# Squared-ReLU attention and a PReLU feed-forward layer on one core: the order of the work written anew, stage by stage

## The chip, the core and the metric

The kernel runs on one core of one Trainium2 chip. A core has five engines that run side by side and wait for each other through semaphores: TensorE (PE in the profile; its weight loads are listed apart as PEld), VectorE (DVE), ScalarE (ACT), GpSimd (POOL) and SyncE (SP). Each engine takes its own instructions strictly in the order in which the program issues them. The metric is device time in microseconds, the median of several executions; less is better.

## The reference

Eight batches, twelve heads, 448 positions, head width 64. Then a feed-forward layer over all 8 x 448 = 3584 rows of width 768, inner width 2048:

```python
scores = scale * np.matmul(q, k.transpose(0, 1, 3, 2))
attn = np.maximum(scores, 0.0) ** 2 / S
x = np.matmul(attn, v)          # heads side by side: 3584 x 768
h = x @ w_in
g = np.maximum(h, 0.0) + alpha * np.minimum(h, 0.0)
return g @ w_out
```

There is no softmax: a score is rectified, squared and used.

## The kernel before

Twelve heads make three *quads* of four heads per batch, 24 quads in all (numbers 0 to 23). Rows of a head are split as 64 x 7, so that a quad's scores come in seven *chunks*.

One chunk is made in three steps. `score_mm` (L199) issues four 64x448 products on 64x64 tiles of TensorE (L204) into a pair of PSUM banks. `relu` (L210) rectifies them into an `rl` buffer, on ScalarE (L213, letter A) or VectorE (L215, letter D). `square` (L218) squares that into an `at` buffer, on VectorE (L226) or ScalarE (L224). A chunk that is rectified but not squared stands in the list `late`; `sq(k, eng)` squares the first k of it. There are six `rl` and ten `at` buffers.

When a quad's seven chunks are squared, `attnv` (L229) multiplies them with v: 28 products on 64x64 tiles (L236) into a pair of banks, which ScalarE (L246) and VectorE (L247) scale into `xT`. Three quads fill `xT` of one batch.

Layer one of the feed-forward part runs in 16 *units* per batch (`f1`, L281): six full-array products (L270) into one bank, then on ScalarE the negative part (L276) and on VectorE the sum (L277) into `gT`, and one square (`sq(1)`).

Layer two works on rows of 128 over two batches. For the first rows it is done plainly (`f2`, L294, products at L301). For the others, `Pair` (L316) computes two row blocks of 128 with seven products of half size instead of eight, from sums and differences of operands (`mix`, L332 on VectorE; `weight_mix`, L314, once for the weights). `p1` to `p7` are the seven products (L336); `p1` and `p2` share a bank that is held in between, as do `p5` and `p3`. Results are added on VectorE (`plus`, L341) or copied on ScalarE (L352, L357), and `store` (L286) writes each piece with two transfers of 64 rows.

q and k of a quad must be transposed. The first five quads are turned on TensorE (`turn_pe`, L171, products at L178, copies at L181). The others are copied into one buffer, `perm`, or a spare part of `w_mix`, on ScalarE or VectorE (L190), and turned by a transfer on SyncE's queue (`turn_dma`, L192). A one-element copy on GpSimd (L508 and others, `landed`) waits for that transfer; the loads that GpSimd issues stand behind it. `prepare` does both and issues the loads of later quads.

PSUM has eight banks. `take_bank` and `take_pair` give out the one or the pair that was taken longest ago; after L652 `one` prefers the neighbour of the bank that was given out last. A bank is free again when the engine that reads it is done.

The order in which all this is issued is written out by hand. Quads 0 to 5 and the first two batches have a list of calls of their own (L413 to L649). From L656 a loop runs over batches 2 to 7. In each batch layer one's 16 units come first, with three chunks before unit 9 (`FB`, L553) and with two quads prepared on ScalarE at units 4 and 12. Then the pairs' products follow, broken by three `burst`s (L565): three chunks, `attnv`, two or three chunks. Squares are issued on VectorE, in groups. At the very start 28 products of the identity with itself (L162) keep TensorE busy until data arrive.

I call a *visit* a run of products on 64x64 tiles (chunks or `attnv`) between full-array products.

Of the kernel before, what the change touches and what calls it, by code (L numbers as in the profile page):

```python
# [10 lines left out]
F32 = mybir.dt.float32  # L11
# [5 lines left out]
NJ = 7  # L17
# [3 lines left out]
def kernel(  # L21
# [43 lines left out]
    beta_sb = singles.tile([128, KF], F32)  # L65
    landed = singles.tile([1, 1], BF16)
# [4 lines left out]
    paired = []  # L71
# [77 lines left out]

    load_k0(0, FIRST)  # L150
# [9 lines left out]
    warm = psum[:, 7, :128]  # L160
    for _ in range(28):
        nc.tensor.matmul(warm, ident, ident, start=True, stop=True)  # L162
# [66 lines left out]
    def attnv(n, eng="AD"):  # L229
# [16 lines left out]
        nc.scalar.activation(xT[b][:, g, 0], ps[:, 0, :S], ACTF.Copy, scale=out_scale)  # L246
        nc.vector.tensor_scalar(xT[b][:, g, 1], ps[:, 1, :S], out_scale, None, ALU.mult)  # L247

    late = []

    def sc(chunks):

        for n, j, eng in chunks:
            late.append((n, j, relu(score_mm(n, j), eng)))

    def sq(k=99, eng="D"):
        for g in late[:k]:
            square(*g, eng)
        del late[:k]

    def run(chunks):
        sc(chunks)
        sq()
# [10 lines left out]
    def f1_out(ps, b, ff):  # L274
        neg = neg_pool.tile([128, S], F32, tag="neg", name="neg")
        nc.scalar.activation(neg, ps, ACTF.Relu, scale=-1.0)  # L276
        nc.vector.scalar_tensor_tensor(gT[:, ff, (b % 2) * S:(b % 2) * S + S],  # L277
                                       neg, beta_sb[:, ff:ff + 1], ps, ALU.mult, ALU.add)
        sq(1)

    def f1(b, ff):  # L281
        ps = take_bank()[:, :S]
        f1_mm(ps, b, ff, range(KM))
        f1_out(ps, b, ff)

    def store(sb, c, lo, hi, t, other=None):  # L286
        for u in range(2):
            blk = 2 * c + u
            b, j = 2 * sb + blk // NJ, blk % NJ
            rows = out[b * S:(b + 1) * S].rearrange("(pp j) d -> j pp d", j=NJ)  # L290
            eng = other if u and other else nc.sync
            eng.dma_start(out=rows[j][:, lo:hi], in_=t[64 * u:64 * u + 64])
# [23 lines left out]
    class Pair:  # L316
# [22 lines left out]
        def plus(self, ps, u, keep=None):  # L339
            t = keep or o_pool.tile([128, d_model - CUT], F32, tag="o", name="osb")[:, :u.shape[-1]]  # L340
# [42 lines left out]

        def p3(self):
# [5 lines left out]
    pat = "ADAAAAA"  # L390

    def ch(n, lo, hi, p=pat):
        return [(n, j, p[j]) for j in range(lo, hi)]

    early = {}
    todo = [(ff, km) for ff in range(4) for km in range(4)]

    def some_early(count):
        for ff, km in todo[:count]:
            if ff not in early:  # L400
                early[ff] = hold()
            f1_mm(psum[:, early[ff], :S], 0, ff, (km,))
        del todo[:count]

    def sq_of(n, j, eng):
        for g in [g for g in late if g[:2] == (n, j)]:
            square(*g, eng)
            late.remove(g)

# [4 lines left out]
    load_w_in(0)  # L414
    load_v(2)
    cast0(0, 2, "D")
    cast0(4, 6, "A")
    cast0(2, 4, "D")
    cast0(6, 7, "A")
    turn_pe(0, (("q", 0, 2, "D"),))  # L420
    turn_pe(0, (("q", 4, 6, "A"),))
    turn_pe(0, (("q", 2, 4, "D"),))
    turn_pe(0, (("q", 6, 7, "A"),))
    turn_pe(0, (("k", 0, 1, "D"),))
    turn_pe(0, (("k", 1, 2, "A"),))
    turn_pe(0, (("k", 2, 4, "D"),))
    sc([(0, 0, "A")])
    sc([(0, 1, "D")])
    turn_pe(0, (("k", 4, 7, "D"),))
    load_qk(3)  # L430
    load_w_in(1)
    load_w_in(2)
    sq_of(0, 0, "D")
    sc([(0, 2, "A")])
    sc([(0, 3, "A")])
    sq_of(0, 1, "D")
    turn_pe(1, (("q", 0, 7, "D"),))
    sc([(0, 4, "A")])
    sc([(0, 5, "A")])
    turn_pe(1, (("k", 0, 7, "D"),))  # L440
    load_qk(4)
    load_w_in(3)
    sq_of(0, 2, "D")
    sq_of(0, 5, "D")
    sc([(0, 6, "A")])
    sq_of(0, 4, "D")
    sq_of(0, 6, "D")
    sc([(1, 0, "A")])
    sq_of(0, 3, "D")
    sc([(1, 1, "A")])  # L450
    sc([(1, 2, "D")])
    sc([(1, 3, "A")])
    sc([(1, 4, "A")])
    sq_of(1, 0, "D")
    turn_pe(2, (("k", 0, 5, "D"),))
    turn_pe(2, (("q", 0, 7, "D"),))
    sq_of(1, 2, "D")
    sq_of(1, 4, "D")
    turn_pe(2, (("k", 5, 7, "A"),))
    load_w_out(0, 0, 8)  # L460
    load_qk(5)
    load_v(3)
    load_w_out(0, 8)
    load_v(4)
    load_v(5)
    sc([(1, 5, "A")])
    sc([(1, 6, "A")])
    sc([(2, 0, "A")])
    sc([(2, 1, "A")])
    sq_of(1, 1, "D")  # L470
    sq_of(1, 5, "D")
    sq_of(1, 3, "D")
    sq_of(1, 6, "D")
    attnv(0, "AD")
    sc([(2, 2, "A")])
    attnv(1, "AD")
    sc([(2, 3, "A")])
    sc([(2, 4, "D")])
    sq_of(2, 0, "A")
    some_early(11)  # L480
    sq_of(2, 4, "A")
    sc([(2, 5, "A")])
    sq_of(2, 1, "D")
    sq_of(2, 3, "D")
    sq_of(2, 2, "D")
    sc([(2, 6, "D")])
    sq_of(2, 5, "A")
    some_early(5)
    sq_of(2, 6, "D")
    nc.vector.tensor_scalar(beta_sb, alpha_sb, -1.0, 1.0, ALU.mult, ALU.add)  # L490
    attnv(2, "AD")
    some_early(0)
    turn_pe(3, (("q", 0, 7, "D"),))
    turn_pe(3, (("k", 0, 7, "D"),))
    for ff in range(4):
        f1_mm(psum[:, early[ff], :S], 0, ff, range(4, KM))
        f1_out(psum[:, early[ff], :S], 0, ff)
        take(early[ff], 1)


    def f1s(b, lo, hi):
        for ff in range(lo, hi):
            f1(b, ff)

    def prepare(n):
        if n < NQ:
            turn_dma(n)
            nc.gpsimd.tensor_copy(landed, T[n][:1, 0, 0, :1])  # L508
# [4 lines left out]

    f1s(0, 4, 6)
    sc(ch(3, 0, 3))
    f1s(0, 6, 8)
    sc(ch(3, 3, 6))
    f1s(0, 8, 9)
    ps = take_bank()[:, :S]
    f1_mm(ps, 0, 9, range(KM))  # L520
    turn_pe(4, (("q", 0, NJ, "A"), ("k", 0, NJ, "D")))
    f1_out(ps, 0, 9)
    f1s(0, 10, 12)
    sc(ch(3, 6, 7) + ch(4, 0, 2, "AA"))
    turn_dma(5, "D")
    f1s(0, 12, 13)
    kept = late[:]
    del late[:]
    f1s(0, 13, 16)
    late += kept  # L530
    nc.gpsimd.tensor_copy(landed, T[5][:1, 0, 0, :1])
    load_qk(6)
    load_qk(7)
    load_qk(8)
    load_w_out(1, 0, 4)
    f2(0, 0, 0)
    sq()
    sc(ch(4, 2, 5, "AAADAAA"))
    attnv(3)
    sc(ch(4, 5, 7, "AAAAAAD"))  # L540
    sq(3)
    sq(2, "A")
    sq()
    f2(0, 1, 0)
    f2(0, 2, 0)
    sc(ch(5, 0, 3))
    sq(1)
    attnv(4)
    sc(ch(5, 3, 5, "AAAADAA"))
    sq()  # L550


    FB = {9: (3, "AAA")}  # L553
    PA = ("ADA", "AAA")
    PB = ("ADA", "AAA")
    PC = ("ADA", "AAA")
    chunks = [(n, j) for n in range(2 * NG, NQ) for j in range(NJ)]
    at_c = [0]

    def some(k, p="ADA"):  # L560
        lo = at_c[0]
        at_c[0] = min(lo + k, len(chunks))
        return [(n, j, e) for (n, j), e in zip(chunks[lo:at_c[0]], p)]

    def burst(n, before="ADA", after="AD", squares=True, mid=0):  # L565

        sc(some(len(before), before))
        sq(mid)
        attnv(n)
        sc(some(len(after), after))  # L570
        if squares:
            sq()

    early = []
    for ff in range(5):
        early.append(hold())
        f1_mm(psum[:, early[ff], :S], 1, ff, range(4))
        if ff == 1:
            sc(ch(5, 5, 7))
            sq(1)  # L580
            sq(1, "A")
        if ff == 3:
            attnv(5)
            turn_dma(6, "D")
            nc.gpsimd.tensor_copy(landed, T[6][:1, 0, 0, :1])
            load_w_out(1, 4)
            load_v(6)
    for ff in range(KF):
        if ff < 5:
            f1_mm(psum[:, early[ff], :S], 1, ff, range(4, KM))  # L590
            f1_out(psum[:, early[ff], :S], 1, ff)
            take(early[ff], 1)
        else:
            f1(1, ff)
        if ff == 9:
            sc(some(3, "AAA"))
        if ff in (1, 8):
            turn_dma(7 + ff // 8, "D")
        if ff == 10:
            nc.gpsimd.tensor_copy(landed, T[8][:1, 0, 0, :1])  # L600
            load_qk(9)
            load_v(7)
            load_qk(10)
            load_v(8)
    p, r = Pair((0, 3), (0, 4)), Pair((0, 5), (0, 6))
    p.p1()
    run(some(3, "AAA"))
    r.p1()
    run(some(2, "AD"))
    p.p2()  # L610
    weight_mix(0, 0, 4)
    r.p2()
    weight_mix(0, 4, 8)
    f2(0, 0, 1)
    weight_mix(1, 0, 4)
    burst(6, "ADA", "AA", False)
    turn_dma(9)
# [153 lines left out]
```

## Time and profile before

| | us |
|---|---|
| median of 3 runs (375.83 to 376.03) | 375.85 |
| the profiled execution, its own time | 376.17 |
| its span, first to last instruction | 374.4 |
| TensorE busy | 364.6 |
| VectorE busy | 289.0 |
| ScalarE busy | 242.1 |
| rectification on ScalarE, mean of one (141) | 0.925 |
| rectification on VectorE, mean of one (27) | 1.090 |
| square on VectorE, mean of one (162) | 0.620 |
| square on ScalarE, mean of one (6) | 0.968 |

How to read it: "busy" is the time in which an engine had an instruction under way. Matmuls overlap and their ends are modelled, so a TensorE that is busy all the time may still be slowed by waits and switches inside; the distance from one row's start to the next row's start tells those. A row such as `L204 ... x12` gathers twelve instructions that follow one another. In brackets stands the idle time of the engine before it, and what ended it. In a table by windows the numbers in turn are the window, its length, the busy time of PE, PEld, DVE, ACT and POOL, the TensorE clock that was granted (1 is full), the share of the DMA engines and GB/s.

### The profile page before, as it was taken

How to read it: one execution, taken by the hardware profiler on the slowest of the kernel's cores; microseconds unless marked ns; L12 is line 12 of the kernel's file. 1: busy time of each engine (PE TensorE's matmuls, PEld its weight loads, DVE VectorE, ACT ScalarE, POOL GpSimd, SP SyncE). 2: the span in 40 equal slices, each digit the busy share in tenths (PEclk: the TensorE clock that was granted, in tenths of full speed). 3: DMA queues.
4: the chain of work that ended last, by engine and by line, in shares of the span. 5: the costliest groups of instructions: out<-in, count | busy, mean ns of one | idle time of the engine just before them, and what ended most of it. 6: DMA issues, size and time to landing. Idle time of an engine off the chain costs nothing.

```text
span 374.4 us, 7851 instructions
## 1 busy us (share of the span) xinstructions
PE 364.6 (97%) x3085; PEld 203.2 (54%) x3088; DVE 289.0 (77%) x481; ACT 242.1 (65%) x369; POOL 72.4 (19%) x120
## 2 busy tenths in 40 slices
PE   6899999999999999999999999999999999999995
PEld 5454574454454566545655456554655556555553
DVE  2988988878978789679796787967876867966753
ACT  4988786766857875685757757577748766424400
POOL 8566150304220222021020220202200000000000
PEclk9899999999999999999999999999999999999999
DMA  9999979999999767537692467925694201220024
GB/s 147 187 203 202 193 115 193 165 156 178 163 166 148 119 106 141 110 63 112 122 178 68 73 105 132 169 63 88 110 156 100 49 2 42 66 65 0 0 65 107
DMA packets 73558, 43.29 MB, mean 116 GB/s; under 512 B 40368, under 2 KB 73008, under 8 KB 73520
## 3 DMA queue, kind: packets, MB, share of 16 engines
q0 software_dynamic: 27136, 22.58, 41.3%
q1 hardware_dynamic: 45952, 19.91, 25.8%
q8 instruction: 24, 0.39, 0.4%
q10 hardware_dynamic: 432, 0.30, 0.3%
q14 instruction: 14, 0.11, 0.1%
HBM read 45.62 MB, written 11.01 MB: 151 GB/s over the span
## 4 chain that ended last, share of the span: by engine, by line
PE 68%; ACT 2%; DVE 1%; issue 0%; DVEq 0%
PE psum L270 29%; PE psum L336 26%; PE psum L236 6%; PE psum L204 5%; PE psum L301 1%; ACT xT L246 1%; DVE osb L341 0%; ACT rl L213 0%; DVE at L226 0%; DVE u L341 0%; DVE S L332 0%; DVEq L341 0%
## 5 line engine op out<-in xcount | busy, mean ns | idle before, releaser
L270 PE MATMUL psum<-xT,w_in_sb 128*128 128x448 bf16 x768 | 149.4, 353 | 0.5 <-DVE gT L277 0.2
L213 ACT ACTIVATE rl<-psum 128x896 bf16<-128x896 f32 x141 | 120.4, 925 | 35.6 <-PE psum L204 35.6
L277 DVE SCALAR_TENSOR_TENSOR gT<-neg,beta_sb,psum 128x448 bf16<-128x448 f32 x128 | 85.3, 678 | 41.2 <-ACT neg L276 40.0
L270 PEld LDWEIGHTS <-w_in_sb 128*128 128x128 bf16 x768 | 73.9, 98 | 73.0 <-issue 6.4
L226 DVE TENSOR_TENSOR at<-rl 128x896 bf16<-128x896 bf16 x162 | 95.7, 620 | 1.8 <-ACT rl L213 1.7
L276 ACT ACTIVATE neg<-psum 128x448 f32<-128x448 f32 x128 | 68.0, 550 | 40.7 <-PE psum L270 33.1
L336 PEld LDWEIGHTS <-S 128*128 128x128 bf16 x384 | 37.2, 98 | 26.7 <-issue 2.7
L336 PE MATMUL psum<-w_mix,S 128*128 128x384 bf16 x288 | 49.2, 326 | 0.2
L204 PE MATMUL psum<-T 64*64 64x448 bf16 x672 | 47.7, 363 | 1.5 <-DVE T L181 0.7
L336 PEld LDWEIGHTS <-gT 128*128 128x128 bf16 x296 | 28.5, 98 | 19.1 <-issue 0.9
L236 PE MATMUL psum<-at,vraw 64*64 64x448 bf16 x672 | 37.1, 352 | 0.3 <-DVE osb L341 0.3
L215 DVE TENSOR_SCALAR rl<-psum 128x896 bf16<-128x896 f32 x27 | 29.4, 1090 | 10.1 <-PE psum L204 8.6
L336 PE MATMUL psum<-w_out_sb,gT 128*128 128x384 bf16 x192 | 33.2, 326 | 0.0
L508 POOL COPY landed<-T 1x1 bf16<-1x1 bf16 x13 | 2.7, 210 | 157.0 <-DMA T<-perm 157.0
L204 PEld LDWEIGHTS <-T 64*64 64x64 bf16 x672 | 19.9, 106 | 22.0 <-issue 15.4
L236 PEld LDWEIGHTS <-vraw 64*64 64x64 bf16 x672 | 23.6, 107 | 11.7 <-issue 4.2
L341 DVE TENSOR_TENSOR osb<-psum,u 128x384 f32<-128x384 f32 (+2 forms) x37 | 20.2, 546 | 8.7 <-PE psum L336 3.9
L247 DVE TENSOR_SCALAR xT<-psum 128x448 bf16<-128x448 f32 x24 | 15.0, 625 | 10.2 <-PE psum L236 7.9
L301 PE MATMUL psum<-w_out_sb,gT 128*128 128x256 bf16 (+1 forms) x125 | 21.7, 325 | 0.2
L357 ACT COPY osb<-psum 128x384 f32<-128x384 f32 x12 | 5.7, 479 | 20.9 <-PE psum L336 20.9
L246 ACT ACTIVATE xT<-psum 128x448 bf16<-128x448 f32 x24 | 13.2, 549 | 8.0 <-PE psum L236 7.3
L123 POOL DMA_DIRECT2D vraw<-in_v_dram x24 | 17.6, 732 | 1.7 <-DMA w_out_sb<-in_moe_w_out_dram 0.6
(47 smaller groups left out, 231.7 us busy)
## 6 DMA issues: line engine op xcount, KB each, us to landing
out_dram<-osb SPq DMA_DIRECT2D x94, 96.0 KB, 2.6
vraw<-in_v_dram POOLq DMA_DIRECT2D x24, 224.0 KB, 6.0
qraw<-in_q_dram POOLq DMA_DIRECT2D x23, 224.0 KB, 4.3
kraw<-in_k_dram POOLq DMA_DIRECT2D x23, 224.0 KB, 5.3
w_in_sb<-in_moe_w_in_dram POOLq DMA_DIRECT2D x16, 192.0 KB, 8.4
w_out_sb<-in_moe_w_out_dram POOLq DMA_DIRECT2D x4, 512.0 KB, 9.8
w_out_sb<-in_moe_w_out_dram POOLq DMA_DIRECT2D x4, 256.0 KB, 8.8
out_dram<-osb SPq DMA_DIRECT2D x8, 128.0 KB, 2.8
```

Of the source, the lines that this page charges most:

```text
L123: nc.gpsimd.dma_start(out=t.rearrange("p m j d -> p m (j d)"), in_=flat[:, 2 * g:2 * g + 2])
L204: nc.tensor.matmul(ps[64 * c:64 * c + 64, r, :S], t[64 * r:64 * r + 64, 1, j, 64 * c:64 * c + 64], t[64 * r:64 * r + 64, 0, :, 64 * c:64 * ...
L213: nc.scalar.activation(rl, ps[:, :, :S], ACTF.Relu)
L215: nc.vector.tensor_scalar(rl, ps[:, :, :S], 0.0, None, ALU.max)
L226: nc.vector.tensor_tensor(a, rl, rl, ALU.mult)
L236: nc.tensor.matmul(ps[64 * s:64 * s + 64, r, :S], vv[64 * r:64 * r + 64, s, j, :], a[64 * r:64 * r + 64, s], start=(j == 0), stop=(j == NJ ...
L270: nc.tensor.matmul(ps, w_in_sb[:, km // 2, km % 2, bass.ts(ff, 128)], xT[b][:, km // 2, km % 2, :], start=(km == 0), stop=(km == KM - 1))
L276: nc.scalar.activation(neg, ps, ACTF.Relu, scale=-1.0)
L277: nc.vector.scalar_tensor_tensor(gT[:, ff, (b % 2) * S:(b % 2) * S + S], neg, beta_sb[:, ff:ff + 1], ps, ALU.mult, ALU.add)
L301: nc.tensor.matmul(ps, gT[:, ff, bass.ts(c, 128)], w_out_sb[:, ff, first_col + lo:first_col + hi], start=(ff == 0), stop=(ff == KF - 1))
L336: nc.tensor.matmul(ps, left[:, i], right[:, i], start=(start and i == 0), stop=(i == KH - 1), skip_group_check=not start)
L341: nc.vector.tensor_tensor(t, ps, u, ALU.add)
```

## The change

The arithmetic stays as it is. The calls that issue the work are replaced by plans: strings of words that `Walk` carries out one by one. A word starts with a letter: `c` chunks, one for each letter of an engine behind it (`cAAD` is three); `s` squares the chunk at a place in the list of waiting ones, on the engine named (`s0D` the first, on VectorE; `s1A` the second, on ScalarE); `v` the value products of the next quad; `f` a unit of layer one (without the square); `p` and `r` a step of the first or second pair (`pa` to `pd` the mixes, `p1` to `p7` the products); `g` a plain piece of layer two; `n` the preparation of the next quad (`nD` with the copies on VectorE); `w` weight mixes, `t` and `d` turnings, `l` the landing copy, `L` loads, `i` warm-up products, `B` the next batch, `z` the switch to two queues for the last stores.

What this does to the engines, by the lists of instructions: squares on VectorE 162 to 116, on ScalarE 6 to 52; rectifications on ScalarE 141 to 121, on VectorE 27 to 47; copies for turning on ScalarE 30 to 20 and on VectorE 8 to 18; warm-up products 28 to 31, and six more behind the first transposes. GpSimd's queue holds the same instructions in the same order. SyncE's has 109 stores and loads instead of 114.

```diff
+    idle = singles.tile([128, 128], BF16)
+    nc.vector.memset(idle, 1.0)
     load_k0(0, FIRST)
...
-    warm = psum[:, 7, :128]
-    for _ in range(28):
-        nc.tensor.matmul(warm, ident, ident, start=True, stop=True)
+    def warm(count):
+        for _ in range(count):
+            nc.tensor.matmul(psum[:, 7, :128], idle, idle, start=True, stop=True)
+    warm(31)
...
+    def chunk(eng):
+        if stream:
+            n, j = stream.pop(0)
             late.append((n, j, relu(score_mm(n, j), eng)))
+    def sq(i, eng):
+        if i < len(late):
+            square(*late.pop(i), eng)
...
                                        neg, beta_sb[:, ff:ff + 1], ps, ALU.mult, ALU.add)
-        sq(1)
...
     def store(sb, c, lo, hi, t, other=None):
+        if last_pair:
+            b, j = 2 * sb + 2 * c // NJ, 2 * c % NJ
+            rows = out[b * S:(b + 1) * S].rearrange("(pp j) d -> j pp d", j=NJ)
+            last_pair[0].dma_start(out=rows[j:j + 2, :, lo:hi], in_=t)
+            last_pair.append(last_pair.pop(0))
+            return
...
+    def prepare(n, eng="A"):
+        if n < NQ:
+            turn_dma(n, eng)
+            land(n)
         if n + 2 < NQ:
             load_qk(n + 2)
         if n + 1 < NQ:
             load_v(n + 1)
...
-    for b in range(2, B):
-        for ff in range(KF):
-            if not last:
-                if ff in FB:
-                    sc(some(*FB[ff]))
-                if ff in (4, 12):
-                    prepare(n0 + 2 + ff // 8)
...
-                r.p2()
-                burst(n0, *PA, False)
-                prepare(n0 + 4)
-                sq(3)
...
+    walk("""Li0 Lv2 x02D x46A x24D x67A t0q24D t0q02D i6 t0q46D t0q67D t0k01A t0k12D t0k24D Lq3 cD cA t0k47D Li1 cA s1D Li2 s0D t1q07D cA cA cA Lq4 t1k07D s1D Li3 s1D cA s0D s1D cA cA s0D t2q07D cA s1D cD cA t2k05D s2D s0D Lo0,0,8 Lq5 Lv3 Lo0,8 cA t2k57A Lv4 s1D s0D Lv5 cA cA s0D cA s0D vDA cA v cA cD s0A e1 e4 s0D cA cD e1 s1A s0D e6 e2 s1A e2 s0D s0D vDA b t3q07A t3k07D E E E E""")
+    walk("""f f cADA f s0D f s1D s0D cADA f t4q07A t4k07D m o f s0D f cAAA s0D s1D d5D f f s0D f l5 Lq6 f Lq7 Lq8 g00 Lo1,0,4 s0D cADA s2D vDA cDD s3D s0D s0A g20 s0A g10 s0D cADA v s0D cAA s0D s1D s0D s0D""")
...
+    walk("""cADA s1D p1 s0D r1 cAD p2 w00 s0D s0A w01 w11 g01 r2 s0D cAD w10 v cDAA d9A l9 Lq11 Lv9 s0D s0A s0D pa w20 g11 cAAA s0D pb pc s1D s1A s0D g21 w21 s0D cADA s0D w30 vDA w31 d10A cA l10 cA p6 Lq12 Lv10 pd s3A s0D p7 Lv11 p5 p4 s0D s0D cAA p3 cD v cADD""")
...
+    EACH = """B s0D f f s0D f f f s1A nD f f f cAAD s1D s0A f s0D f f s0A s1A p1 f f f f f r1 n pc s0D p2 r2 cA pa ra pb cD vDA cA s0D p6 s0D n cAA s0D pd cA p7 rc s1A s0A p5 p4 p3 cAAD rb v cADA s2D s1A s3A r6 s0A s0D s0A rd r7 cDAA r5 r4 s0D r3 cD v cAA"""
+    ONE_PAIR = """B f f nD s0A s1D s0A s2D f f s0D f s0A f f f f f cAD s0D s0D cA f s0D n f f f f f pa pc g50 pb cADA s0A vDA p1 cDAA s0D p2 p6 s0A s1D p7 s0A pd n p5 p4 p3 cADA s1D s0D v cAA s0D s1D cD s2D s1D g51 s0D cADA v cA cDA"""
+    LAST = """B f f s1A s5D f f f f f f s2A f s0D f s0D s0D f f f f f f pa p1 pc r1 pb p2 p6 pd ra p7 p5 rc rb p4 p3 r6 z rd r7 r5 r2 r3 r4e"""
+    for b, plan in ((2, FIRST_PAIR), (3, EACH), (4, EACH), (5, ONE_PAIR), (6, EACH), (7, LAST)):
```

`FIRST_PAIR`, for batch 2, is built like `EACH`; its visits are `cDDA`, then `cADA v cAAA`, `cADA vDA`, `cDAA`, `cAAD` and `cA v cAA`. `r4e` is the fourth product in two parts, of columns 0 to 256 and 256 to 384, as before.

## The prediction

> **What bounds the kernel now.** I read the page's first two parts, then busy time by window, then TensorE's timeline, where the start of one row to the start of the next is the only fair measure, since a matmul's end is modelled and rows overlap.
>
> ```profile
> span 374.4 us, 7851 instructions
> PE 364.6 (97%) x3085; PEld 203.2 (54%) x3088; DVE 289.0 (77%) x481; ACT 242.1 (65%) x369; POOL 72.4 (19%) x120
> PEclk9899999999999999999999999999999999999999
> ```
>
> ```profile
> 0.00:10.00 10.00, 7.18 (x94) 5.35 (x94) 3.27 (x9) 4.85 (x9) 8.36 (x17) 1.00 1.01 150
> 10.00:20.00 10.00, 8.17 (x135) 5.05 (x131) 10.00 (x20) 9.79 (x14) 5.60 (x9) 0.83 1.21 188
> 20.00:30.00 10.00, 9.94 (x122) 5.19 (x115) 8.61 (x15) 8.06 (x13) 6.16 (x10) 1.00 1.24 203
> ```
>
> The columns are window, length, then PE, PEld, DVE, ACT, POOL busy, clock, DMA. TensorE is short of work only in the first 20 us; from 10 to 20 VectorE (10.00) and ScalarE (9.79) are both full and set the pace. After that TensorE never stands: so nothing behind 20 us is to be won from the other engines as such, only from what TensorE itself loses inside its rows.
>
> ```profile
> 2.71 3.17 PE L162 MATMUL psum<-ident 128*128 128x128 bf16 x28 [2.71 <-POOL ident masks.py:199]
> 5.81 0.96 PE L178 MATMUL psum<-ident,qraw 128*64 128x128 bf16 x14
> 6.56 0.63 PE L178 MATMUL psum<-ident,kraw 128*64 128x128 bf16 x8
> 7.20 0.91 PE L204 MATMUL psum<-T 64*64 64x448 bf16 x8
> ```
>
> The 28 warm-up products wait for the identity (2.71) and end only at 5.81, though the first q lands at about 4.0 (0.74 + 3.3 in the DMA issues) and the first k at about 5.84 (1.24 + 4.6). The first scores come at 7.20.
>
> ```profile
> 34.48 0.76 PE L204 MATMUL psum<-T 64*64 64x448 bf16 x12
> 35.18 2.44 PE L270 MATMUL psum<-xT,w_in_sb 128*128 128x448 bf16 x12
> 37.55 0.58 PE L178 MATMUL psum<-ident,qraw 128*64 128x128 bf16 x14
> ...
> 164.65 1.09 PE L204 MATMUL psum<-T 64*64 64x448 bf16 x12
> 165.68 8.12 PE L270 MATMUL psum<-xT,w_in_sb 128*128 128x448 bf16 x42
> 173.63 5.36 PE L336 MATMUL psum<-w_out_sb,gT 128*128 128x384 bf16 x32
> 178.92 0.76 PE L204 MATMUL psum<-T 64*64 64x448 bf16 x12
> 179.52 1.56 PE L236 MATMUL psum<-at,vraw 64*64 64x448 bf16 x28
> 180.84 0.80 PE L204 MATMUL psum<-T 64*64 64x448 bf16 x12
> 181.64 4.06 PE L336 MATMUL psum<-w_mix,S 128*128 128x384 bf16 x24
> ```
>
> These price a visit (score or value products on 64x64 tiles between full-array products). The 28 value products take 180.84 - 179.52 = 1.32, or 0.189 for each four; a chunk of scores is four, so three chunks are 0.57. At 34.48 three chunks alone take 0.70: 0.13 too much on the way out. The 12 full products behind them take 2.37, against 12 x 7.95/42 = 2.27: 0.10 on the way in. A lone visit costs 0.23. At 164.65 the same visit takes 1.03, 0.33 more: a PSUM wait inside the row, seen also at 121, 211, 257 and 299 (1.02 each in the chain). Three chunks, values, three chunks take 181.64 - 178.92 = 2.72 against 2.46: 0.26 over, and 2.86 (0.40 over) at 188.23 and 197.68, so 0.35 in the mean, 0.45 with the way in.
>
> ```profile
> 369.78 1.11 SPq L292 DMA_DIRECT2D out_dram<-osb  x2
> ...
> 371.62 0.55 SPq L292 DMA_DIRECT2D out_dram<-osb  x1
> ```
>
> At the end the last piece is computed at 370.75 (VectorE row at 370.01, 0.74 long) but its store is issued at 371.62: it stands behind other stores in SyncE's queue.
>
> **The change part by part.** The sum is made against the profiled execution: 376.17 us, a span of 374.4 and 1.77 around it. It stands 0.32 above the median of 375.85, which I take off at the end.
>
> *Start.* The cleared tile needs one VectorE fill. The trace has none on VectorE: it lies between the 0.17 of a small VectorE row and the 0.22 of POOL's fill, and before 4.0 VectorE is idle. TensorE can begin at about 1.0 (queues open at 0.74); 31 products at 0.11 end at 4.4. Then q is transposed while k is under way; six more warm-up products (0.64) lie before k's landing at 5.84, and would cost that 0.64 only if k came earlier. From k's transposes to the first score it was 7.20 - 6.56 = 0.64, so the first score falls at about 6.5, 0.7 earlier. Work behind it is the same: 4 of 21 rectifications on VectorE and 3 squares on ScalarE, as before. Bounds: 0, if loads or the full engines take it back (w_in's first quarter, four POOL transfers of which the last is issued at 10.1 and lands at most 9.6 later, is used at 21.38, so there is 1.7 to spare), and -1.2, if the half clock (0.50 from 14.75 to 18.16, when 3.41 us of TensorE's work was worth 1.7) goes too; ScalarE idles only 0.21 in that window and VectorE not at all, so little of it shows. I take **-0.5**.
>
> The row says half speed early on: 0.11 a warm-up product, and transposes that take 0.96 for 14 at 5.81 but 0.58 at 9.12. The Trainium skill (TensorE: Matmul & The Clock Gate, section Part 1: The HAM clock gate) says that the array starts at half clock and is released after a busy window of 3.4 us that runs free of the kernel. 31 products are 3.3 us, so by the rule they need not fill one window, and the start would win perhaps 0.2 instead of 0.5: the sum would be -2.7 instead of -3.0.
>
> *Second stage, 61 to 111.* TensorE loses inside its rows 0.16 at 72 (a layer-one row released late by VectorE), 0.34 at 100.2 (two chunks take 0.85 to the next row instead of 0.51) and 0.47 at 107.7 (three chunks 1.06 instead of 0.59); VectorE is 9.7 busy of 10 there and its sums (L341) release PSUM late. The new order has one lone visit more (+0.23); it gives ScalarE 4 of the squares (4 x 0.62 off VectorE) but VectorE 4 more rectifications (4 x 1.09). Bounds +0.2 (only the visit) and -0.75 (all waits gone). Words p7 p5 p4 now follow one another with no square between their sums, where one or two stood before, so I take a value near the lower end: **-0.5**.
>
> *Steady stages, 111 to 334.* Before: five lone visits at 0.56 (with the wait), fourteen of 3+values+3 at 0.45, one of values alone 0.24; together 9.3. After, by the words of the plans: thirteen lone visits, six 3+values+3, six with at most two chunks behind the values (at 47.93 such a visit took 2.39 against 2.27, so 0.12 + 0.10), three that end on the values (0.24). The wait of 0.33 goes: before, nine layer-one units precede the chunks, banks 0,1,4,5,6,7,2,3,0, and the third chunk's pair 2,3 holds the eighth unit, still being read; after, eight (or ten) units end on a full pair and the third chunk meets the fifth and sixth. Sum after: 13 x 0.23 + 6 x 0.45 + 6 x 0.22 + 3 x 0.24 = 7.7. Difference **-1.6**; I take -1.5. Bounds: -1.8 and, if the wait stays at each lone visit, +2.7 (13 x 0.33 more).
>
> The rule that speaks against this: the Trainium skill (TensorEngine Tiling (Array Packing), section Key Properties) says that a change of tiling mode drains the array. The 0.23 agrees; if only the drains counted, eight more visits would add 8 x 0.23 = 1.8, and the sum would be +0.3 instead of -3.0.
>
> *Engines.* 52 squares on ScalarE instead of 6: 46 x 0.968 = +44.5 there, -28.5 (x 0.620) on VectorE; 20 rectifications the other way, -18.5 (x 0.925) and +21.8 (x 1.09); ten half-copies of turned q and k to VectorE, -9.5 and +6.1. ScalarE about 259, VectorE about 288 of 371: both stay under TensorE, which hides them. In layer one a unit takes 1.13 of TensorE, 0.55 of ScalarE, 0.68 of VectorE; a square (0.95) makes one unit's output about 0.4 late, and the bank comes round only eight units later, 9 us. Without that cover it would be 0.4 for each of some 20 squares.
>
> *Transfers.* POOL issues the same 96 loads and 18 landing copies in the same order. In each stage the single perm buffer is now filled twice within about 6 us (words n ... n), and the second copy waits on ScalarE for the first transpose to land (4.0, at most 4.8, in 16 from that buffer); behind it stand three rectifications. SyncE has stores queued behind the transposes: six output buffers cover those. Bounds: 0 and the rival below. 0.
>
> *Tail.* The fourth mixed operand is prepared earlier (TensorE's weights waited 0.33 for it at 363.7): **-0.2**, between 0 and -0.33. Last stores: one transfer per piece, alternating queues, so the last can issue at about 370.85 instead of 371.62, -0.77; but they are twice as large (2.8 for 128 KB, 2.4 for 64 KB): the piece before it, out at 370.47, lands at 373.27 instead of 373.48. Between +0.3 and -0.77; **-0.3**.
>
> Sum: -0.5 - 0.5 - 1.5 - 0.2 - 0.3 = -3.0. 376.17 - 3.0 - 0.32 = 372.85.
>
> **The rivals.** (1) The half clock in 14.75 to 18.16 goes too: 0.7 more, 372.2. For it: more transposes between scores. Against: ScalarE and VectorE stay full. (2) The start and the second stage give nothing, since both are set by full VectorE and ScalarE: +1.0, 373.9; for it the 10.00 and 9.79. (3) Slower: a lone visit keeps the bank wait. Thirteen at 0.56 give 13 x 0.33 = 4.3 more, 377.2; it decides from about 9 of 13 on. For it: ScalarE's squares delay the outputs that release banks. Against: the bank order above. (4) The perm wait: a transpose under load (12.0 was seen once, beside the w_out loads) would hold ScalarE some 6 us longer than TensorE's banks allow, in two stages: +12; below about 7 us of landing it costs nothing, and at 7.5 the gain is half gone. That the order is not what the plans say is excluded: the lists of instructions show it.
>
> **How the numbers follow.** Forecast 0.62 (its own range 371.9 to 374.0); (1) 0.12; (2) 0.12; (3) 0.08; (4) 0.06, half of it near no change. A run of this kernel tells 0.2% (0.75 us) from no change: faster is below 375.1. The forecast, (1) and (2) are faster: 0.86, of which 0.02 is taken off for a bad end of (2); within 0.05; slower 0.11. The range leaves out most of (3) and (4) and the far end of (1): 371.5 to 375.2.
>
> **What would show it.** Warm-up from about 1.0 and first scores near 6.5; layer one of the first batch under way 0.5 earlier; in the steady stages lone three-chunk rows of 0.70 everywhere, none of 1.02, and a stage of the third batch 0.3 shorter than 46.2; the last store issued within 0.2 of the last VectorE row. Wrong if lone visits show 1.0, if ScalarE is the releaser of score rows, or if the copies into perm wait over 2 us.

## The result, and the profile after

The changed kernel takes 387.21 us (median of 5 runs, 386.35 to 387.73) against 375.94 us (5 runs, 375.83 to 376.13): 1.0295 times the time before, 95% interval 1.0277 to 1.0312. It is 11.3 us slower where 3.0 us faster was forecast. The profiled execution took 386.44, of which the span is 384.7; against the profiled execution of before (376.17, span 374.4) it is 10.3 more, and the table below accounts for these 10.3. It was among the faster of the five.

The page of the changed kernel, its first two parts:

```profile
span 384.7 us, 7874 instructions
PE 363.6 (95%) x3097; PEld 196.8 (51%) x3097; DVE 291.3 (76%) x467; ACT 257.2 (67%) x384; POOL 73.9 (19%) x120
...
PE   7899999999999999999999999999999999999920
...
DMA  9999999989799989084982469766652012200311
```

Each digit stands for 9.6 us. TensorE's row is 9 up to the last two slices and ends in 2 and 0. Before, it stayed in work to the last slice. So nothing was lost in the middle; some 17 us at the end have no computing in them, and in them the DMA row says 1, a tenth busy, not idle.

The end by windows (window, length, busy PE, PEld, DVE, ACT, POOL, clock, DMA share, GB/s), first the kernel before, then the changed one:

```profile
368.00:370.00 2.00, 2.00 (x19) 1.52 (x18) 0.56 (x1) 0.32 (x1) 0.00 (x0) 1.00 0.61 144
370.00:372.00 2.00, 0.42 (x8) 0.24 (x5) 0.72 (x2) 0.00 (x0) 0.00 (x0) 1.00 0.62 148
372.00:374.40 2.40, 0.00 (x0) 0.00 (x0) 0.00 (x0) 0.00 (x0) 0.00 (x0) 0.74 0.32 85
```

```profile
366.00:368.00 2.00, 1.80 (x19) 1.40 (x17) 1.15 (x3) 0.00 (x0) 0.00 (x0) 1.00 0.13 31
368.00:370.00 2.00, 0.00 (x0) 0.00 (x0) 0.13 (x1) 0.00 (x0) 0.00 (x0) 1.00 0.13 41
...
376.00:378.00 2.00, 0.00 (x0) 0.00 (x0) 0.00 (x0) 0.00 (x0) 0.00 (x0) 0.50 0.13 49
...
382.00:384.70 2.70, 0.00 (x0) 0.00 (x0) 0.00 (x0) 0.00 (x0) 0.00 (x0) 0.50 0.06 18
```

TensorE's last row ends at 367.80 (1.80 busy from 366), before at 370.42: the computing is 2.62 earlier, as forecast (2.7 without the last stores). Then the stores run, before at a DMA share of 0.61 and 144 GB/s, after at 0.13 and some 50 GB/s to the end. 0.13 of 16 DMA engines is two engines, and the share stays at 0.13 to 0.14 from 366 to 382. The five last stores carry 3 x 192 + 128 + 64 = 768 KB (786 kB); at 50 GB/s that is 15.7 us.

### The profile page after: what moved, and what is told of

Its sections match the earlier page's. It is cut to its first block, busy times and chain, and to the rows that moved or that the text cites. A ratio compares the mean times of both kernels' runs of the same rounds, so it can differ in the third digit from the quotient of the medians.

```text
span 384.7 us, 7874 instructions
## 1 busy us (share of the span) xinstructions
PE 363.6 (95%) x3097; PEld 196.8 (51%) x3097; DVE 291.3 (76%) x467; ACT 257.2 (67%) x384; POOL 73.9 (19%) x120
## 4 chain that ended last, share of the span: by engine, by line
PE 89%; ACT 3%; DVE 2%; issue 1%; DMA 1%; ACTq 0%
PE psum L275 36%; PE psum L341 29%; PE psum L209 8%; PE psum L241 8%; PE psum L306 6%; ACT rl L218 2%; DVE gT L282 1%; PE psum L183 1%; DMA qfirst<-in_q_dram 1%; ACT xT L253 1%; ACT neg L281 1%; DVE w_mix L195 1%; DVE qraw L412 0%; PE psum L165 0%; DVE osb L346 0%
## 5 line engine op out<-in xcount | busy, mean ns | idle before, releaser
L275 PE MATMUL psum<-xT,w_in_sb 128*128 128x448 bf16 x768 | 149.9, 353 | 0.3 <-DVE gT L282 0.2
L218 ACT ACTIVATE rl<-psum 128x896 bf16<-128x896 f32 x121 | 104.7, 923 | 14.9 <-PE psum L209 11.3
L275 PEld LDWEIGHTS <-w_in_sb 128*128 128x128 bf16 x768 | 73.5, 98 | 73.5 <-issue 6.7
L231 DVE TENSOR_TENSOR at<-rl 128x896 bf16<-128x896 bf16 x116 | 68.8, 618 | 0.5 <-ACT rl L218 0.2
L220 DVE TENSOR_SCALAR rl<-psum 128x896 bf16<-128x896 f32 x47 | 50.7, 1085 | 5.5 <-PE psum L209 4.8
L341 PE MATMUL psum<-w_mix,S 128*128 128x384 bf16 x288 | 50.0, 326 | 0.2
L209 PE MATMUL psum<-T 64*64 64x448 bf16 x672 | 46.8, 362 | 2.0 <-ACT rl L218 1.9
L229 ACT ACTIVATE at<-rl 128x896 bf16<-128x896 bf16 x52 | 47.4, 950 | 0.1
L424 POOL COPY landed<-T 1x1 bf16<-1x1 bf16 x18 | 5.7, 315 | 208.0 <-DMA T<-perm 184.1
L209 PEld LDWEIGHTS <-T 64*64 64x64 bf16 x672 | 17.4, 106 | 23.3 <-issue 16.6
L241 PEld LDWEIGHTS <-vraw 64*64 64x64 bf16 x672 | 21.6, 108 | 12.0 <-issue 2.9
```

The source lines that it names most:

```text
L209: nc.tensor.matmul(ps[64 * c:64 * c + 64, r, :S], t[64 * r:64 * r + 64, 1, j, 64 * c:64 * c + 64], t[64 * r:64 * r + 64, 0, :, 64 * c:64 * ...
L218: nc.scalar.activation(rl, ps[:, :, :S], ACTF.Relu)
L220: nc.vector.tensor_scalar(rl, ps[:, :, :S], 0.0, None, ALU.max)
L229: nc.scalar.activation(a, rl, ACTF.Square)
L231: nc.vector.tensor_tensor(a, rl, rl, ALU.mult)
L241: nc.tensor.matmul(ps[64 * s:64 * s + 64, r, :S], vv[64 * r:64 * r + 64, s, j, :], a[64 * r:64 * r + 64, s], start=(j == 0), stop=(j == NJ ...
```

## Where each term of the sum stands

Since layer one is the first work of each stage, the start of its first row (L270 before, L275 after) in the second, third and eighth batch cuts the span where the prediction cut it:

| piece | before | after | change | forecast |
|---|---|---|---|---|
| span's start to layer one, second batch | 56.32 | 55.39 | -0.93 | -0.5 |
| to layer one, third batch | 54.56 | 54.05 | -0.51 | -0.5 |
| to layer one, eighth batch | 222.86 | 221.81 | -1.05 | -1.5 |
| to the end of TensorE's last row | 36.68 | 36.55 | -0.13 | -0.2 |
| from there to the end of the span | 4.0 | 16.9 | +12.9 | -0.3 |

Four terms out of five hold within half a microsecond. The fifth is wrong by 13 us and decides. The experiments ask first what makes those stores slow, and then whether the four good numbers came about for the reasons given.

## Experiments: the last stores

**The old stores in the new order.** The word that turns the new stores on is taken out of the last plan:

```diff
-    LAST = """... p4 p3 r6 z rd r7 r5 r2 r3 r4e"""
+    LAST = """... p4 p3 r6 rd r7 r5 r2 r3 r4e"""
```

> The changed kernel with the last stores issued as before the change (two transfers of 64 rows for each piece, all but the last on SyncE's queue); the rest of the new order stays. Theory S (the new stores alone made it slower; a store of two blocks of 64 rows is carried by 2 of the 16 DMA engines, as the DMA share of 0.13 after 368 says): the rows on TensorE end at 367.8 as in the changed kernel, and from there it is 4.0 us to the end of the span as in the kernel before, so a span of 371.8 and a time of 373.2 to 373.6, 2.3 to 2.7 faster than before. Theory Q (the tail is slow because ScalarE's queue takes part, or because something else of the new order holds DMA): the tail stays over 10 us, time above 380. Theory C (the new order's gain of 2.6 at the last TensorE row is partly borrowed from later work): time of 375 or more.

Measured: 373.62 (373.25 to 374.83), ratio 0.9948 (0.9932 to 0.9965). This is what theory S says, at the upper edge of its range: the gain of the order was there all the time.

**The new stores in the old order.**

```diff
+        if last_pair:
+            b, j = 2 * sb + 2 * c // NJ, 2 * c % NJ
+            rows = out[b * S:(b + 1) * S].rearrange("(pp j) d -> j pp d", j=NJ)
+            last_pair[0].dma_start(out=rows[j:j + 2, :, lo:hi], in_=t)
+            last_pair.append(last_pair.pop(0))
+            return
...
+            if last:
+                last_pair.extend((nc.sync, nc.scalar))
```

> The kernel before with nothing changed but the last pair's five stores, in the new form (one transfer for each piece of 128 rows, alternating between SyncE's and ScalarE's queue). Theory S: TensorE's last row stays at 370.4, the stores take 16.9 us behind it instead of 4.0, so 12.9 slower: 388 to 389.5. Theory Q with the new order as a partner: under 380.

Measured: 388.83 (388.1 to 388.92), ratio 1.0341 (1.0327 to 1.0355). TensorE's last row ends at 370.24, the span at 387.1: 16.9 behind it, as in the changed kernel. The stores do it alone, whatever order stands before them.

**All five on one queue.**

```diff
-                last_pair.extend((nc.sync, nc.scalar))
+                last_pair.extend((nc.sync, nc.sync))
```

> The changed kernel with its five new stores all on SyncE's queue. Theory S (two DMA engines because the written rows are two blocks; both queues use the same two): the bytes and the engines are the same, so the time stays within 1 us of the changed kernel's 387.2, and the DMA share in the tail stays at 0.13. Rival (each queue feeds one DMA engine): one engine is left, the DMA share falls to 0.06 and the tail doubles, about 400. Rival (the two queues disturb each other): faster than the changed kernel by several us.

Measured: 386.55 (386.51 to 386.62), ratio 1.0285 (1.0271 to 1.0298). A window of its tail:

```profile
376.00:378.00 2.00, 0.00 (x0) 0.00 (x0) 0.00 (x0) 0.00 (x0) 0.00 (x0) 0.50 0.13 51
```

The share is 0.13 with one queue as with two. So it is not one DMA engine for each queue, which would have given 0.06 here. Nor had each queue a pair of its own in the changed kernel, since with stores waiting on both queues the share would have been 0.25. The transfers of both queues went through the same two engines, and a second queue brings no bandwidth.

**Two queues, but transfers of 64 rows.**

```diff
-            last_pair[0].dma_start(out=rows[j:j + 2, :, lo:hi], in_=t)
-            last_pair.append(last_pair.pop(0))
+            for u in range(2):
+                last_pair[u].dma_start(out=rows[j + u][:, lo:hi], in_=t[64 * u:64 * u + 64])
```

> The changed kernel with two queues kept for the last stores, but each piece stored as two transfers of 64 rows, the first half on SyncE's queue and the second on ScalarE's. Theory S: every transfer is spread over the 16 DMA engines again, and each queue has only one issue of about 0.55 for a piece, so the last store is issued at about 368.2 rather than some 0.8 later: 372.3 to 373.2, up to 0.8 faster than the run with the old stores. Rival Q: over 380.

Measured: 373.28 (372.96 to 374.57), ratio 0.9940 (0.9924 to 0.9956). Its tail:

```profile
366.00:368.00 2.00, 1.59 (x18) 1.26 (x16) 1.27 (x3) 0.00 (x0) 0.00 (x0) 1.00 0.48 138
368.00:370.00 2.00, 0.00 (x0) 0.00 (x0) 0.00 (x0) 0.00 (x0) 0.00 (x0) 1.00 0.73 197
370.00:371.30 1.30, 0.00 (x0) 0.00 (x0) 0.00 (x0) 0.00 (x0) 0.00 (x0) 0.50 0.00 0
```

The same bytes from the same tiles over the same two queues are through at about 370. From TensorE's last row to the end it takes 3.7 (367.60 to 371.3), with the old stores 3.98 (367.95 to 371.93). In all the profiles it is 3.71 to 3.74 with halves (five runs) and 3.97 to 3.99 with the old stores (four runs). The idea of two queues was sound and worth about 0.25, too little for the two medians (373.28 and 373.62) to show; the shape of the transfer spoiled it.

**62 rows and 2.** Is it the two blocks in one transfer, or the number of rows that come first in its pattern?

```diff
-                last_pair[u].dma_start(out=rows[j + u][:, lo:hi], in_=t[64 * u:64 * u + 64])
+                for r0, r1 in ((0, 62), (62, 64)):
+                    last_pair[u].dma_start(out=rows[j + u][r0:r1, lo:hi], in_=t[64 * u + r0:64 * u + r1])
```

> The new order with the last stores by halves on two queues, but each half of 64 rows stored as a transfer of 62 rows and one of 2. It asks what sets the number of DMA engines. If it is the number of rows in the outermost dimension, 2 being the largest number up to 16 that divides 62, all these bytes go by two engines again: DMA share 0.13 in the tail and 385 to 388, though no transfer has two blocks any more. If it is the pattern of two blocks in one transfer, as theory S was first put, 62 rows spread like 64: the ten issues on each queue of about 0.55 are then the only cost, 373.3 to 375. The Trainium skill (DMA: Bandwidth & Descriptors, section Why a DMA increments its semaphore by 16 and not by 1) gives the first of these as its rule.

Measured: 386.16 (385.94 to 387.23), ratio 1.0276 (1.0262 to 1.0290).

```profile
376.00:378.00 2.00, 0.00 (x0) 0.00 (x0) 0.00 (x0) 0.00 (x0) 0.00 (x0) 0.50 0.13 50
```

No transfer has two blocks any more, every one is a plain set of rows, and splitting 64 rows into 62 and 2 brings the two engines back. Theory S in its first wording (two blocks) falls; the row count decides. The Trainium skill (DMA: Bandwidth & Descriptors, section Why a DMA increments its semaphore by 16 and not by 1) has the rule: a transfer is split over the largest number of engines, up to 16, that divides the outermost dimension of both its patterns. The runs agree at the three shapes tried: outermost 2 against 128 partitions gives a share of 0.13, 62 rows 0.13, 64 rows up to 0.73. Other counts were not tried.

## Experiments: the order

**The old warm-up in the new order.**

```diff
-            nc.tensor.matmul(psum[:, 7, :128], idle, idle, start=True, stop=True)
+            nc.tensor.matmul(psum[:, 7, :128], ident, ident, start=True, stop=True)
...
-    warm(31)
+    warm(28)
...
-    walk("""... t0q24D t0q02D i6 t0q46D ...""")
+    walk("""... t0q24D t0q02D t0q46D ...""")
```

> The new order with the last stores by halves on two queues, and the warm-up of the kernel before put back: 28 products on the identity (released at 2.7 instead of 1.06), without the six more before the second half of q. It measures the start's term by itself. If the cleared tile is what makes the start earlier, the first layer-one row moves back from about 20.5 (20.08 to 20.82 in four runs with the new start) to about 21.3 (21.26 and 21.38 in two with the old one), and the time rises by 0.5 to 0.9 over the run by halves (373.28), to about 374. If the new order of the first stage does it, the time stays at 373.3 and the row at 20.5.

Measured: 374.12 (373.62 to 374.49), ratio 0.9950 (0.9937 to 0.9962): 0.84 over the run by halves and 0.47 over a second run of the same kernel (373.65, below). The intervals overlap, so the times alone don't settle it. First scores are at 7.24 as before the change, and the first layer-one row is at 21.64, so the new order of the first stage does not make the start earlier by itself. What the cleared tile wins differs from run to run. In the changed kernel, and in the second run by halves, the start looked like this (timeline of TensorE):

```profile
1.06 3.29 PE L165 MATMUL psum<-idle 128*128 128x128 bf16 x31 [1.06 <-DVE idle L151]
4.92 0.41 PE L183 MATMUL psum<-ident,qraw 128*64 128x128 bf16 x8 [0.56 <-DVE qraw L412]
...
6.56 0.57 PE L209 MATMUL psum<-T 64*64 64x448 bf16 x8 [0.19 <-ACT T L186]
```

```profile
7.04 0.41 PE L183 MATMUL psum<-ident,kraw 128*64 128x128 bf16 x8 [0.71 <-DMA kraw<-in_k_dram]
7.65 0.57 PE L209 MATMUL psum<-T 64*64 64x448 bf16 x8 [0.19 <-DVE T L186]
```

The load of k took 4.7 from issue to landing in the first and 5.8 in the second, and the scores follow it. Over eight runs with the cleared tile the first scores come at 6.43 to 7.65 (median 7.0) and the first layer-one row at 20.08 to 21.29 (median 20.7). In the five with the identity the scores come at 7.2 every time, and the row at 20.64 to 21.64 (median 21.4). Only two of the eight show a wait for k (0.44 and 0.71). With all squares on VectorE (below) k took 4.7 too and the scores came at 7.19: there the first q was waited for (0.38), and the six more warm-up products took 0.82 instead of 0.51.

So the first scores come 0.2 earlier in the median. The rest of the 0.65 between the two medians of the layer-one row can't be put down to the cleared tile, because the half clock is mixed in. A stretch of 3.41 us at half clock stands between 14 and 18.4 in four of the five profiles with the identity, this one among them, and in one of the eight with the cleared tile, that of the changed kernel. Here it is in this run (the clock is the third number from the end):

```profile
16.00:18.00 2.00, 2.00 (x24) 0.91 (x24) 2.00 (x5) 1.74 (x4) 1.51 (x3) 0.50 1.16 182
```

Both runs by halves have a clock of 1.00 there. With the stretch the layer-one row is at 21.26 to 21.64 with the identity and at 20.51 with the tile; without it, at 20.64 (one run) and at 20.08 to 21.29. In the kernel before the stretch seems to come and go: of 46 executions with a clock on record 22 have a mean clock of 0.993 to 0.995 and 24 one of 0.997 or more, and 3.41 us at half clock are 0.005 of the mean. What decides was not tried. So the worth of the cleared tile stays open: 0.2 by the median of the first scores, 0.9 by the two profiled executions, nothing by the single run with the identity and without the stretch.

**Eight units before the chunks, in the kernel before.** This tests the prediction's cause for the 0.33 lost at each lone visit:

```diff
-    FB = {9: (3, "AAA")}
+    FB = {8: (3, "AAA")}
```

> The kernel before with one number changed: the three chunks inside layer one come after eight units instead of nine, in each of five stages. If the 0.33 lost there is a PSUM pair still being read by the ninth unit's neighbour, the five rows of 1.02 become 0.70 and the last TensorE row comes 5 x 0.33 = 1.6 earlier: 374.2 to 374.5. Rival (the wait belongs to the place in the plan, to VectorE being late, and stays): 375.9, rows of 1.02 as they were.

Measured: 377.05 (376.37 to 377.32), ratio 1.0029 (1.0020 to 1.0038): slower, which neither of the two explanations had forecast. TensorE in the fourth batch:

```profile
163.05 0.76 PE L204 MATMUL psum<-T 64*64 64x448 bf16 x12
164.30 3.94 PE L270 MATMUL psum<-xT,w_in_sb 128*128 128x448 bf16 x20 [0.49 <-DVE gT L277]
```

From start to start the visit now takes 1.25 instead of 1.02, in all five stages. The chunks do find free banks, but the unit behind them wants the bank of the seventh unit, and VectorE has not read it yet (that gT ends at 164.25). The wait moved and grew. So the order of banks only decides who waits; that someone waits has another cause.

**Nine units, but no square behind units 5 to 8.**

```diff
-        sq(1)
+        if not (2 <= b < B - 1 and 5 <= ff <= 8):
+            sq(1)
```

> The kernel before with the order of banks as it was (nine units, then three chunks), but without a square behind the units 5 to 8 of the third to the seventh batch; those squares come behind later units. It tells two causes of the 0.33 at a lone visit apart. Theory V: with a square behind every unit VectorE needs about 1.29 for each 1.13 of TensorE, so gT of the eighth unit is late when the third chunk wants its bank; without those squares gT is on time, the rows of 1.02 become 0.70, and the last TensorE row comes up to 5 x 0.33 = 1.6 earlier: 374.2 to 375. Theory B (the order of banks by itself, as the prediction had it: a bank of the eighth unit is still being read whatever VectorE does): rows of 1.02 stay, 375.9.

Measured: 374.36 (373.87 to 374.52), ratio 0.9957 (0.9944 to 0.9971). TensorE and VectorE of this run, then VectorE of the kernel before in the same stage:

```profile
164.27 0.76 PE L204 MATMUL psum<-T 64*64 64x448 bf16 x12
164.97 3.20 PE L270 MATMUL psum<-xT,w_in_sb 128*128 128x448 bf16 x16
...
162.54 2.03 DVE L277 SCALAR_TENSOR_TENSOR gT<-neg,beta_sb,psum 128x448 bf16<-128x448 f32 x3
```

```profile
157.19 0.68 DVE L277 SCALAR_TENSOR_TENSOR gT<-neg,beta_sb,psum 128x448 bf16<-128x448 f32 x1 [2.77 <-ACT neg L276]
...
162.92 0.68 DVE L277 SCALAR_TENSOR_TENSOR gT<-neg,beta_sb,psum 128x448 bf16<-128x448 f32 x1
163.51 0.62 DVE L226 TENSOR_TENSOR at<-rl 128x896 bf16<-128x896 bf16 x1
164.05 2.03 DVE L277 SCALAR_TENSOR_TENSOR gT<-neg,beta_sb,psum 128x448 bf16<-128x448 f32 x3
```

The visit takes 0.70, in all five stages, with the bank order as it was. Theory V is shown in this: the wait is there because VectorE is late, and it goes when VectorE gets less to do. The 1.29 a unit that theory V gives VectorE is not what the rows say, though, since they overlap: from gT to gT, with a square between, it is 1.13 (162.92 to 164.05), TensorE's own pace. VectorE does not fall behind; it starts late and can't catch up. The first gT of the stage waits 2.77 for ScalarE, which still rectifies three chunks (154.19 to 156.72). It starts 2.85 after its unit's first product, and so does each gT up to the seventh unit's, within 0.06; with no such delay it is 1.91. The gT of the eighth unit then ends at 165.31, and the last two products of the third chunk start at 165.37. Without the four squares it ends at 164.56, before that chunk starts at 164.68. One condition in the old kernel wins 1.6 us, without a new order.

**All squares of the steady stages back on VectorE**, in the new plans (42 of 52):

```diff
-    FIRST_PAIR = """B f s0D ... f f f f s0A cDDA ..."""
+    FIRST_PAIR = """B f s0D ... f f f f s0D cDDA ..."""
...
```

> The new order with the last stores by halves on two queues, with every square of the third to the eighth batch on VectorE: it undoes the split of squares over two engines alone, in the same places of the plans. If engine time is hidden behind TensorE, as the prediction's step of zero has it, the time stays within 0.5 of the run by halves (373.28), since VectorE, 291 busy of 385 in the changed kernel, gets some 15 more and ScalarE gives up some 23. If the split of squares is what lets the smaller visits run without waits, waits come back in the rows of TensorE in the steady stages: 1 to 4 slower, 374.3 to 377.

Measured: 381.21 (380.86 to 382.0), ratio 1.0142 (1.0127 to 1.0158), 7.9 over the run by halves, about twice the most that was expected. TensorE behind a visit of the fourth batch:

```profile
184.77 1.46 PE L341 MATMUL psum<-w_mix,gT 128*128 128x384 bf16 x8
187.00 1.46 PE L341 MATMUL psum<-w_out_sb,S 128*128 128x384 bf16 x8 [0.76 <-DVE osb L346]
...
194.64 1.48 PE L341 MATMUL psum<-w_mix,S 128*128 128x384 bf16 x8
197.22 1.46 PE L341 MATMUL psum<-w_mix,gT 128*128 128x384 bf16 x8 [1.11 <-DVE u L346]
```

Eight such products take 1.3; here 2.2 and 2.6 lie between the starts, since VectorE squares before it does the sums that free the banks. It is busy only 38.49 of 46 us in that stage. A mean of 84% does not say that work is hidden: it is hidden while each sum is on time.

**A version of both**: the new start, second stage and last batch, stores by halves, and in between the old plans with the squares behind units 5 to 8 left out; beside it the run by halves once more.

```diff
-    EACH = """B s0D f f s0D f f f s1A nD f f f cAAD s1D ..."""
+    EACH = """B f s0D f s0D f s0D f s0D n f s0D f f f f cAAA f s0D ... r2 cADA v cAAA n ..."""
...
```

> A version of both: start, second stage and last batch of the new order, last stores by halves on two queues, and between them the old plans of the third to the seventh batch with the squares behind units 5 to 8 left out (as in the run with spaced squares). From the first layer-one row of the third batch to that of the eighth, the spaced old plans took 332.05 - 110.82 = 221.23 and the new plans 331.04 - 109.22 = 221.82, so 0.6 less than the run by halves: 372.5 to 372.9. If the gains do not add (the old plans find another state of PSUM and of waiting squares behind the new second stage), 373.3 or more, with rows of over 0.70 at lone visits.

> The new order with the last stores by halves on two queues once more, beside the version of both, for the difference of the two: as before, 373.28 within 0.4.

Measured: 373.04 (372.82 to 373.25), ratio 0.9928 (0.9916 to 0.9940), and 373.65 (373.1 to 374.14), ratio 0.9943 (0.9929 to 0.9956). Layer one of the third batch to that of the eighth takes 221.22 in the one and 221.80 in the other: the 0.6 adds as expected, and the time is 0.14 over the forecast range. By the times alone the two can't be told apart with certainty. Both beat the kernel before, by 2.9 and 2.3, and the changed kernel by over 13.

## Why the prediction was wrong

- **Last stores (-0.3, "between +0.3 and -0.77"): the step that failed.** It sized the new transfers by their bytes, from rows of 128 KB and 64 KB, as "twice as large". Those rows are transfers whose outermost dimension is 64 rows; the new ones have two blocks outermost, and no row of before showed one. Shape was an unknown that the step did not bound. A bound could be had by asking how many engines carry a transfer: 144 GB/s at a share of 0.61, or 9.8 engines, is 14.8 GB/s for one, and 786 kB over two such would be 27 us; the two gave 25 each and took 16. Measured +12.9. With the shape mended and the queues kept, 0.25 comes out (tail of 3.7 against 3.98 with the old stores), so the argument on the queues held.
- **"What would show it: the last store issued within 0.2 of the last VectorE row."** It was issued at 368.16, 0.03 behind the last VectorE row, and the kernel was slow all the same. The forecast looked at the issue and not at the landing.

```profile
367.39 0.74 DVE L346 TENSOR_TENSOR osb<-psum,u 128x256 f32<-128x256 f32 x2 [0.26 <-PE psum L341]
...
368.16 0.99 SPq L289 DMA_DIRECT2D out_dram<-osb  x1
```

- **Start (-0.5, bounds 0 and -1.2): the cause open in part.** In the two profiled executions, both with the half clock, layer one of the first batch came 0.87 earlier. Of this 0.64 are the first scores, at 6.56 where 6.5 was forecast. Over all runs the first scores gain 0.2 in the median, which is what the prediction's sentence on the clock gate left; the half clock, which the sum kept out, blurs the rest. In the changed kernel the warm-up products stand 0.107 apart until 4.02 and then 0.056, 2.96 after the first of them. In the seven other runs with the cleared tile all 31 stand at the slow distance (3.49 in all). Both occur, and no run here shows what decides.
- **Second stage (-0.5): measured -0.51.** Of the two visits that were to lose their waits, the one before layer one (1.06) has none any more, and the one at 100.2 (0.85) takes 0.65 at 99.24. The 0.16 at 72 stayed (at 71.17).
- **Steady stages (-1.5): -1.05, with the wait's place right and its cause wrong.** All thirteen lone visits run at 0.69 to 0.70 from start to start, as forecast. In the kernel before, the third chunk does wait for the eighth unit's bank. But what makes that wait is VectorE being late, as the run with spaced squares shows, and not "the bank order above". The new plans have no square behind every unit, and the gT of the last unit before the visit inside layer one starts 1.91 after its unit in all five stages. The copies of the first quad on VectorE are not needed for it: the third batch still makes them on ScalarE, and its visit takes 0.69 too. It also follows that the sentence "nothing behind 20 us is to be won from the other engines as such" was too strong: 1.6 us came from VectorE's list alone. The size missed in visits with values. Counted as the prediction counts, the six of 3 + values + 3 lose 0.37 each on the way out instead of 0.35, those with fewer chunks behind the values 0.13 instead of 0.12, and one that ends on the values waits 0.15 more: some 0.3 over the forecast. The old plans' fourteen lost 0.34 instead of 0.35, so there was some 0.2 less to win.
- **Tiling changes.** If only the drains counted, the computing would have been 0.6 slower (the sum of +0.3 without the stores' -0.3), not 2.6 faster. A lone visit still costs 0.23. By the prediction's prices the five waits of 0.33 that went (1.65) nearly pay for the eight lone visits more (1.84); the gain comes from the visits with values, which are fewer or shorter (6.5 before, 4.7 after).
- **Engines (0): true one way only.** 46 squares more on ScalarE cost nothing that TensorE's rows show in the steady stages. Putting 42 of them back on VectorE costs 7.9 in these plans; in the version of both, VectorE makes all squares of the third to the seventh batch at other places, and nothing is lost.
- **Transfers (0) and rival 4:** ScalarE's copies wait twice for the transpose, 1.1 us in all, the longest 0.6, and VectorE's once, 0.5, so rival 4 did not occur:

```profile
ACT perm L195 <- DMA T<-perm: 1.1, 2, 0.6
```

- **Rival 1:** the half clock stayed in the profiled execution (0.63 in 14 to 15, 0.50 to 17, 0.67 to 18). It is absent from the profiles of the seven other runs with the new start, but from one with the old start too, so that the change takes it away is not shown. **Rival 3**, the slower one, named the wrong place: no lone visit kept its wait. None of the rivals looked at where the bytes of a store go.

## What to carry to other kernels

Size a new transfer by its pattern before its bytes: look at which dimension comes outermost on both sides and whether a row of the profile has moved that shape, and read the DMA share in the tail (0.13 is two engines of 16). When several edits come together, take the cheap suspicious one out first: one word of the plan turned +11.3 into -2.5. And before a wait is put down to an order of buffers, see whether the engine that frees the buffer is simply late; moving the consumer (1.25 instead of 1.02) made it worse, unloading that engine (0.70) removed it. Starts of different runs are compared with the granted clock beside them.

## What the runs showed that was not expected

- Two DMA engines move 45 to 51 GB/s, some 25 each, with rows of 0.5 to 1.5 KB; with 64 rows outermost the same stores run at up to 197 GB/s.
- Transfers of 62 rows and 2 instead of 64 cost 12.9 us over ten halves (386.16 against 373.28).
- A second queue changed nothing for such transfers (386.55 on one, 387.21 on two).
- Eight runs with the same new start have first scores 1.2 us apart (6.43 to 7.65), with landings of k at 4.5 to 5.8 and warm-up at two speeds, while five with the old start have them at 7.18 to 7.24.
- An engine with exactly the pace of the one it serves (1.13 a unit) carries a delay of 0.94 from the first unit to the seventh without losing any of it.
